# Spreading a first loop's loads over its instruction order, piece by piece, and shortening the warming ahead of the next loop

## The chip, the cores and the metric

The kernel runs on one core of one Trainium2 chip. A core has five engines that run side by side: TensorE (PE in the profile, with its weight loads as PEld), VectorE (DVE), ScalarE (ACT), GpSimd (POOL) and SyncE (SP), which here only issues DMAs. Each engine takes its instructions in the order in which the program gives them; between engines there are only semaphores. The metric is the time of one execution in microseconds (us) on the device, as the median of several runs.

## The reference

Two blocks in a row, in fp32. The first is a linear attention with a decaying state (RWKV-6). For each of 4 batches and 8 heads, over 768 steps of head dimension 48:

```python
for t in range(S):
    cur = einsum('bhd,bhe->bhde', u[None] * k[t], v[t])
    y[t] = einsum('bhd,bhde->bhe', r[t], state + cur)
    state = w[t][..., None] * state + einsum('bhd,bhe->bhde', k[t], v[t])
```

The second is a two-layer network on the 3072 tokens of width 384 that come out of it, with the exact gelu:

```python
h = x @ w_in            # 384 -> 2048
g = 0.5 * h * (1 + erf(h / sqrt(2)))
out = g @ w_out         # 2048 -> 384
```

The weights arrive as float64, so the kernel also converts them to fp32 on the chip.

## The kernel before, in words

**Tiles.** The work is cut into eight tiles of 384 steps (x = 0 to 7; two tiles for each batch). One pass of the outer loop, number x, does the attention of tile x, and beside it the network of tile x - 1. So the first pass, "the first loop" below, has attention alone, and it does it in two units, each with half of the heads, to start before all of its data is there. The second pass starts with the first h products (`first_mlp`, line 1084), each followed by a gelu on ACT (line 1086) that frees one of two PSUM banks which the h products use in turn.

**Order.** Nothing is scheduled by a tool. Every part of the kernel is a Python generator that emits a few instructions and yields; a string `PLAN[x]` says by its letters which generator goes on next. In pass 0 they are: "." and "s" the two units, "l" the loads, "c" the conversion of weights, "p" early conversion steps on ACT, "w" the load of the next tile's v, "f" the beginning of tile 1's attention, "x" the warming of TensorE. As every engine works in order, a letter's place fixes where its instructions stand on each engine.

**Loads.** SP issues nearly all of them, on one queue:
- `load_first` (line 274): tile 0's r, k, w, six DMAs of 384 KB, unit 0's three first. No mark.
- `load_v` (line 278): a tile's v in one DMA of 584 KB. All tiles share one buffer for it.
- `load_second` (lines 285, 286): tile 1's r, k, w in eight DMAs of 288 KB.
- `weight_in` (lines 322, 326, 327): a piece of the weights, 768 KB of float64, into one of five buffers `raw`. With `gate` it goes in three DMAs of 256 KB, without it in one.
- `load` (line 298): the r, k, w and v of later tiles.

**Marks.** In `load_second`, and in `weight_in` with its gate, each DMA is preceded by a memset of one column of its target on DVE. The DMA writes the same bytes, so it has to wait for the memset, and so it is issued not before DVE's order has come to that place. Everything behind it on SP waits too.

```python
nc.vector.memset(bufs[1][:, s.start:s.start + 1], 0.0)
dma.dma_start(out=bufs[1][:, s], in_=rkw[1, :, s])
```

**Conversion.** For a piece, three ACT instructions (lines 459, 460, 462, `prepare`) read `raw`; two DVE instructions (471, 475, `finish`) make the fp32 weights; then the load three pieces further on is issued without a mark. The second "p" of pass 0 prepares piece 2; this stands on ACT ahead of the first gelu.

**Ends of pass 0.** Unit 1's result goes from PSUM to SBUF on ACT (line 970), and from there in six small DMAs into xT (line 886, three issued by SP, three by ACT). Then tile 1 begins: sums on DVE (534), r times u on ACT (524, tile kx), products on PE (575). The warming is a set of bf16 matmuls on zeros (`keep_warm`, line 349), two times three of 512 columns, between those products.

Of the kernel before, what the change touches and what calls it, by code (L numbers as in the profile page):

```python
# [10 lines left out]
F32 = mybir.dt.float32  # L11
# [25 lines left out]
NC_SP = 8  # L37
HALFWAY = 2
PLAN = {
    0: "l.s....llsl.lssslslss.lc.l.slslls...ssss..lcs.s.s.l.ss..ss..sccs.c.s.llpssslw..cs.ffpccxx",  # L40
    1: (
        "swcs.clc.cs.wccscwcc.csccsw..cwlsccccccsc.cs.swcccc.ccc.s.cwlssccsclcs.cwss.lscccsw.c.cwcw"
        ".s..clw..lw..wwccc..cccc.scc.l.cslfccscfccw.fcffy.w.y..fw....ywyw..yyxxx.wyfxx..x.w..y.fyx"
# [149 lines left out]
def kernel(  # L193
# [9 lines left out]
    nc = tc.nc  # L203
# [12 lines left out]
    io = ctx.enter_context(tc.tile_pool(name="io", bufs=2))  # L216
# [8 lines left out]
    def pair(name):  # L225
        return pools["d"].tile([128, 2, BANK], F32, name=name, tag="d")

    def fewer_pairs():
        pairs_of_banks.close()
        pools["d"] = ctx.enter_context(tc.tile_pool(name="pe", bufs=2, space=PSUM))  # L230
        pools["u"] = ctx.enter_context(tc.tile_pool(name="pu", bufs=1, space=PSUM))
        for i in range(2):
            u = bank_u(i)
            nc.tensor.matmul(u, lhsT=zeros[:, 0:128], rhs=zeros, start=True, stop=True)
# [6 lines left out]
    def bank(name="o_ps", i=None):  # L241
        if i is None:
            i = turns[0]
            turns[0] = 1 - i
        return ps.tile([128, BANK], F32, name=name, tag=f"m{i}")
# [4 lines left out]
    loaded = {}  # L250

    def units_of(x):
        return NPART if x == 0 else 1
# [4 lines left out]
    bufs = [io.tile([128, 3 * NP * T], F32, name=f"rkw{i}", bufs=1) for i in range(2)]  # L258
# [7 lines left out]
    def load_first():  # L266

        t = bufs[0]
        loaded[0] = [None, None]
        size = 3 * NP * T // units_of(0)  # L270
        nc.scalar.dma_start(out=u_sb, in_=u)
        for i, part in ((0, 2), (0, 0), (0, 1), (1, 0), (1, 1), (1, 2)):
            s = slice(i * size + part * size // 3, i * size + (part + 1) * size // 3)
            nc.sync.dma_start(out=t[:, s], in_=rkw[0, :, s])

    def load_v(x, dma):
        loaded[x][1] = io.tile([128, v.shape[2]], F32, name="v_in", bufs=1)
        dma.dma_start(out=loaded[x][1], in_=v[x])

    def load_second(dma):  # L280

        loaded[1] = [None, None]
        for i in range(SHARES):
            s = slice(i * 3 * ALL // SHARES, (i + 1) * 3 * ALL // SHARES)
            nc.vector.memset(bufs[1][:, s.start:s.start + 1], 0.0)
            dma.dma_start(out=bufs[1][:, s], in_=rkw[1, :, s])
            yield

    def load(x, dma):

        if x >= NX:
            return
        loaded[x] = [None, None]
        for i in (0, 2, 1):
            t = bufs[x % 2 if i == 0 else 1]
            for j in range(3):
                a = i * ALL + j * ALL // 3
                dma.dma_start(out=t[:, a:a + ALL // 3], in_=rkw[x, :, a:a + ALL // 3])
                yield
        load_v(x, dma)  # L300
        yield
# [12 lines left out]
    def weight_in(i, gate=False):  # L314

        if i < len(pieces):
            dst, src = pieces[i]
            raws[i] = cv.tile([128, PIECE], I64, name="raw", bufs=AHEAD) if wide else None
            if wide:
                dst = raws[i].rearrange("p (a c) -> p a c", a=dst.shape[1])  # L320
            if not gate:
                nc.sync.dma_start(out=dst, in_=src)
                return
            for a in range(dst.shape[1]):
                if wide:
                    nc.vector.memset(dst[:, a].bitcast(U32)[:, 0:1], 0)
                nc.sync.dma_start(out=dst[:, a], in_=src[:, a])
                yield

    load_first()  # L330
    load_v(0, nc.sync)


    zeros = const.tile([128, BANK], BF16, name="zeros")
# [8 lines left out]
    def keep_warm(n, elsewhere=False, n_cols=BANK):  # L343
        if elsewhere:
            t = pair("warm")[:, 0]
        else:
            t = bank("warm")
        for _ in range(n):
            nc.tensor.matmul(t[:, 0:n_cols], lhsT=zeros[:, 0:128], rhs=zeros[:, 0:n_cols], start=True, stop=True)
# [698 lines left out]
    def h_sums(qs):  # L1048

        for q in qs:  # L1050
            for o, sign, a, b in FORMS_W:
                o, a, b = (of_q(w_block(z), q) for z in (o, a, b))
                (nc.vector.tensor_add if sign == "+" else nc.vector.tensor_sub)(o, a, b)
                yield
# [7 lines left out]
    def sums_of_x(x):  # L1062

        for o, sign, a, b in FORMS_X:
            o, a, b = (x_form(z) for z in (o, a, b))
            if sign == "n":
                nc.vector.scalar_tensor_tensor(out=o, in0=a, scalar=-1.0, in1=b, op0=ALU.mult, op1=ALU.subtract)
            else:
                (nc.vector.tensor_add if sign == "+" else nc.vector.tensor_sub)(o, a, b)
            yield  # L1070
# [7 lines left out]
    def first_mlp():  # L1078

        gs = [gp.tile([128, FG, T], F32, name="g") for _ in range(NF // FG)]  # L1080
        for f in range(NF):
            h_ps = bank("h_ps")[:, 0:T]
            for j in range(NJ):
                nc.tensor.matmul(h_ps, lhsT=w_in_sb[:, f // FI, j, f % FI * 128:(f % FI + 1) * 128], rhs=xT[:, j, :],  # L1084
                                 start=(j == 0), stop=(j == NJ - 1))
            nc.scalar.activation(out=gs[f // FG][:, f % FG], in_=h_ps, func=AF.Gelu)
            yield
        for blocks in (0, 1), (2,):
            o_ps = {i: bank()[:, 0:DM] for i in blocks}
            for f in range(NF):  # L1090
                for i, o in o_ps.items():
                    nc.tensor.matmul(o, lhsT=gs[f // FG][:, f % FG, i * 128:(i + 1) * 128], rhs=w_out_sb[:, f, :],  # L1092
                                     start=(f == 0), stop=(f == NF - 1))
                if f < NF - 1:
                    yield
            for i, o in o_ps.items():
                o_sb = wk.tile([128, DM], F32, name="o_sb", bufs=OUTS)
                nc.scalar.copy(out=o_sb, in_=o)
                store(i * 128, o_sb)
            yield  # L1100
# [139 lines left out]
    second = load_second(nc.sync)  # L1240
# [8 lines left out]
    def prepare_apart():  # L1249
        for i in range(2, 2 + HALFWAY):  # L1250
            prepare(i)
            yield

    def next_v():
        load_v(1, nc.sync)
        yield

    def warm():
        for _ in range(2):
            keep_warm(3, True)  # L1260
            yield

    def masks_and_sums():
        yield from make_quarter_masks()
        homes()
        yield from h_sums([0])
# [3 lines left out]
    for x in range(NX):  # L1270
        following = attention(x + 1, 0) if x + 1 < NX else iter(())
        if x == 0:
            streams = {
                ".": units[0], "s": units[1], "f": following, "c": pieces_of_w, "w": next_v(), "x": warm(),
                "p": prepare_apart(),
                "l": chain(weight_in(0, True), islice(second, 5), weight_in(1, True), second, weight_in(2, True)),
            }
        else:
            streams = {
                **(mlp(x - 1) if x > 1 else {".": first_mlp()}),  # L1280
                "s": slots, "f": following,
                "l": load(x + 1, nc.sync),
                "x": sums_of_x(x),
                "w": masks_and_sums() if x == 1 else chain(h_sums([1]), o_sums(EARLY, len(FORMS_O))) if x == 2 else iter(()),
                "y": o_sums(0, EARLY) if x == 1 else iter(()),
                "c": pieces_of_w if x == 1 else iter(()),
            }
        for c in PLAN[x]:
            next(streams[c], None)
        for c in ".slxwp" if x == 0 else ".slxwcy" if x == 1 else ".vgeoslxw":  # L1290
            while next(streams[c], streams) is not streams:
                pass
        slots = following
        if x == 1:
            fewer_pairs()
# [63 lines left out]
```

## Time and profile before

| what | value |
|---|---|
| median of 3 runs | 576.1 us (575.36 to 579.16) |
| the profiled execution | 577.52 us, span 575.7 us |
| PE busy | 551.3 us (96%) |
| DVE busy | 489.2 us (85%) |
| ACT busy | 334.1 us (58%) |
| PE's clock as granted | 1.00 |
| DMA, mean over the span | 108 GB/s; 303, 178 and 159 in the first three slices of 14.4 us |
| first h product on PE | 42.58 us |

The profile shows one execution, in microseconds from its start. A row of the timeline gives start, length, engine, line, operation, the tile written and the tiles read, and in brackets for how long the engine had been idle and what released it. "SPq" and "ACTq" rows are DMA issues, "issue" as a releaser means that the engine waited for nothing that the profile shows. The order of SP's issues in pass 0 is, with their starts: r, k, w of tile 0 (0.74 to 3.1), v (3.57), w_in piece 0 (4.51, 9.21, 9.63), five parts of tile 1 (10.10 to 15.36), w_in piece 1 (16.47 to 18.67), the other three parts of tile 1 (19.15, 24.44, 26.66), piece 3 without a mark (27.04), two parts of piece 2 (31.20, 31.63), three moves into xT (36.60), the third part of piece 2 (38.57), v of tile 1 (39.23).

### The profile page before, as it was taken

The page shows a single profiled execution, that of the slowest core. Times are in us where ns is not written, and L with a number is a line of the kernel's source. Part 1 is how long each engine was busy: PE and PEld are TensorE (multiplying, and loading weights), DVE is VectorE, ACT ScalarE, POOL GpSimd, SP SyncE. Part 2 cuts the span into 40 slices and gives each one's busy share as a digit, 9 for nine tenths or more (in the row PEclk, how much of TensorE's full clock was granted, in tenths as well). Part 3 has the DMA queues.
Part 4 walks back from the last instruction along what each step waited for, and adds up shares of the span by engine and source line. Part 5 has one row for each costly group of instructions (what it writes and reads, how often), then busy time and mean ns, then how long its engine had stood idle before and what let it go on. Part 6 is the DMA issues. An engine that isn't in the chain of part 4 may idle for free. (4 is left out here: it accounts for less than half of the span.)

```text
span 575.7 us, 17712 instructions
## 1 busy us (share of the span) xinstructions
PE 551.3 (96%) x7412; PEld 491.1 (85%) x7420; DVE 489.2 (85%) x977; ACT 334.1 (58%) x768; POOL 106.1 (18%) x105
## 2 busy tenths in 40 slices
PE   7689999999998999999999999999999999999997
PEld 4576665689998989999898998989898988999997
DVE  7889879999989989798989979799888989755464
ACT  2468995347753677347763477527772478535820
POOL 5100000016200460006400252005500072000000
PEclk9999999999999999999999999999999999999999
DMA  8559742239342782558623593337915384200001
GB/s 303 178 159 370 239 142 87 81 86 154 47 82 64 175 106 36 139 156 131 81 46 114 135 165 44 60 91 159 131 30 135 84 105 62 43 25 30 0 1 41
DMA packets 71646, 62.15 MB, mean 108 GB/s; under 512 B 32912, under 2 KB 56720, under 8 KB 71568
## 3 DMA queue, kind: packets, MB, share of 16 engines
q1 hardware_dynamic: 50112, 45.62, 26.4%
q0 software_dynamic: 21216, 15.34, 20.3%
q8 instruction: 58, 0.95, 0.7%
q14 instruction: 20, 0.16, 0.1%
q10 hardware_dynamic: 240, 0.08, 0.1%
HBM read 36.24 MB, written 4.72 MB: 71 GB/s over the span
## 5 line engine op out<-in xcount | busy, mean ns | idle before, releaser
L1148 POOL DMA_DIRECT2D g<-o_sb x78 | 94.9, 1490 | 370.7 <-ACT g L1117 347.2
L1197 DVE TENSOR_TENSOR g<-g 128x512 f32<-128x512 f32 x112 | 75.1, 688 | 24.3 <-PE o_ps L1073 21.3
L1117 ACT COPY o_sb<-u_ps 128x384 f32<-128x384 f32 (+1 forms) x56 | 25.8, 461 | 67.6 <-PE u_ps L1073 66.2
L1073 PE MATMUL h_ps<-forms_x,w_in_sb 128*128 128x192 f32 x280 | 57.7, 332 | 0.0
L1073 PE MATMUL o_ps<-w_out_sb,g 128*128 128x192 f32 x280 | 50.5, 327 | 0.5 <-DVE g L1197 0.5
L1117 ACT COPY g<-h_ps 128x384 f32<-128x384 f32 x84 | 40.4, 482 | 16.3 <-PE h_ps L1073 14.4
L1073 PEld LDWEIGHTS h_ps<-forms_x,w_in_sb 128*128 128x128 f32 x280 | 46.6, 190 | 2.7 <-ACT g L1117 2.2
L1073 PEld LDWEIGHTS o_ps<-w_out_sb,g 128*128 128x128 f32 x280 | 46.0, 190 | 1.2 <-DVE g L1197 0.8
L1166 ACT ACTIVATE g<-g 128x384 f32<-128x384 f32 x98 | 46.2, 519 | 0.3
L1073 PE MATMUL o_ps<-t,g 128*128 128x192 f32 x224 | 41.4, 328 | 0.1
L726 ACT COPY a_sb<-d 32x320 f32<-32x320 f32 (+5 forms) x108 | 39.3, 364 | 3.6 <-DVE a_sb L784 1.7
L1073 PEld LDWEIGHTS o_ps<-t,g 128*128 128x128 f32 x224 | 36.8, 190 | 0.7 <-PE u_ps L1073 0.3
L1073 PE MATMUL h_ps<-forms_x,s 128*128 128x192 f32 x168 | 35.5, 334 | 0.0
L1073 PE MATMUL h_ps<-xT,w_in_sb 128*128 128x192 f32 x168 | 35.0, 331 | 0.1
L710 PE MATMUL d<-kx,rkw 64*64 64x96 f32 x1152 | 32.0, 248 | 3.0 <-ACT a_sb L726 1.9
L710 PEld LDWEIGHTS d<-kx,rkw 64*64 64x64 f32 x1152 | 25.6, 133 | 9.6 <-issue 4.3
L1084 PE MATMUL h_ps<-xT,w_in_sb 128*128 128x384 f32 x96 | 33.0, 494 | 0.2
L1073 PE MATMUL u_ps<-xT,w_in_sb 128*128 128x192 f32 x168 | 32.5, 328 | 0.1
L1073 PE MATMUL u_ps<-w_out_sb,g 128*128 128x192 f32 x168 | 30.9, 332 | 1.4 <-ACT o_sb L1115 0.8
L1092 PE MATMUL o_ps<-w_out_sb,g 128*128 128x384 f32 x96 | 31.7, 489 | 0.0
L575 PEld LDWEIGHTS d<-rkw 64*64 64x64 f32 x1152 | 19.1, 134 | 14.2 <-issue 8.5
L739 DVE COPY_PREDICATED a_sb<-quarter,d 128x480 f32<-128x480 uint8 (+5 forms) x54 | 23.2, 440 | 8.7 <-PE d L710 7.4
(178 smaller groups left out, 1206.2 us busy)
## 6 DMA issues: line engine op xcount, KB each, us to landing
g<-o_sb POOLq DMA_DIRECT2D x78, 192.0 KB, 4.2
rkw<-in_rkw_dram SPq DMA_DIRECT2D x54, 256.0 KB, 3.7
raw<-in_w_out_dram SPq DMA_DIRECT2D x8, 768.0 KB, 5.4
v_in<-in_v_dram SPq DMA_DIRECT2D x8, 584.0 KB, 4.6
out_dram<-o_sb SPq DMA_DIRECT2D x24, 192.0 KB, 2.1
raw<-in_w_in_dram SPq DMA_DIRECT2D x5, 768.0 KB, 9.2
rkw<-kx SPq DMA_DIRECT2D x72, 48.0 KB, 2.1
rkw<-in_rkw_dram SPq DMA_DIRECT2D x6, 384.0 KB, 6.8
```

The source lines that it names most:

```text
L575: nc.tensor.matmul(d[half[p], g, n * width:(n + 1) * width], lhsT=kc[half[g], b, i, p], rhs=right(half[g], b, i, p), start=True, stop=True)
L710: nc.tensor.matmul(d[half[p], g, i * 3 * C // 2:(i + 1) * 3 * C // 2], lhsT=kc[half[g], n // NI, n % NI, p], rhs=rx[half[g], 2 * n + p], s ...
L726: nc.scalar.copy(out=at[z, g, first:behind, (a + 1) * h:], in_=d[z, :, :, to] if g == slice(None) else d[z, :, to])
L739: nc.vector.copy_predicated(out=an[:, :, :, :, (a + 1) * h:], mask=mask.to_broadcast(data.shape), data=data)
L1073: nc.tensor.matmul(o, lhsT=lhsT, rhs=rhs, start=start, stop=True, skip_group_check=True)
L1084: nc.tensor.matmul(h_ps, lhsT=w_in_sb[:, f // FI, j, f % FI * 128:(f % FI + 1) * 128], rhs=xT[:, j, :], start=(j == 0), stop=(j == NJ - 1))
L1092: nc.tensor.matmul(o, lhsT=gs[f // FG][:, f % FG, i * 128:(i + 1) * 128], rhs=w_out_sb[:, f, :], start=(f == 0), stop=(f == NF - 1))
L1117: nc.scalar.copy(out=o, in_=z)
L1148: nc.gpsimd.dma_start(out=o, in_=saved[q, t], accum_op=ALU.add)
L1166: nc.scalar.activation(out=o, in_=z, func=AF.Gelu, scale=MINUS.get(h, 1.0))
L1197: nc.vector.tensor_add(o, o, g_block(what[3:5]))
```

## The change

Three edits:
- v of tile 0 is no longer issued right behind r, k, w. It comes in two halves of 292 KB, each with a mark, out of the "l" stream, between w_in piece 0 and tile 1's r, k, w.
- The plan of pass 0 has two "l" more, and all of them stand elsewhere. The order of all other letters is the same: with the "l" taken out, both strings read alike. Counted in other letters that stand ahead of it, the loads are begun at:

| load | before | after |
|---|---|---|
| w_in piece 0, three parts | 0, 6, 6 | 6, 8, 11 |
| v of tile 0 | ahead of all | 12, 15 |
| tile 1, first five parts | 7, 8, 11, 12, 15 | 17, 19, 22, 24, 27 |
| w_in piece 1 | 17, 19, 20 | 30, 36, 38 |
| tile 1, last three parts | 20, 30, 37 | 41, 51, 55 |
| w_in piece 2 | 55, 55, 59 | 59, 62, 65 |

  "w", which loads tile 1's v, is letter 59 (so a load at 59 stands ahead of it, one at 62 behind), "p" are letters 55 and 67, "f" 65 and 66, and the "c" that issues piece 3 is 51.
- The warming in "x" takes 64 columns in place of 512.

```diff
-    0: "l.s....llsl.lssslslss.lc.l.slslls...ssss..lcs.s.s.l.ss..ss..sccs.c.s.llpssslw..cs.ffpccxx",
+    0: ".s....ls.lssslslss.lc.l.slss.l..lsssls..lcs.s.sl..lss.l.ss..sccs.lc.s.lpssslw..lcs.lffpccxx",
...
+    def first_v():
+        loaded[0][1] = t = io.tile([128, v.shape[2]], F32, name="v_in", bufs=1)
+        for i in range(2):
+            s = slice(i * v.shape[2] // 2, (i + 1) * v.shape[2] // 2)
+            nc.vector.memset(t[:, s.start:s.start + 1], 0.0)
+            nc.sync.dma_start(out=t[:, s], in_=v[0][:, s])
+            yield
+
     load_first()
-    load_v(0, nc.sync)
...
         for _ in range(2):
-            keep_warm(3, True)
+            keep_warm(3, True, 64)
             yield
...
-                "l": chain(weight_in(0, True), islice(second, 5), weight_in(1, True), second, weight_in(2, True)),
+                "l": chain(weight_in(0, True), first_v(), islice(second, 5), weight_in(1, True), second, weight_in(2, True)),
```

## The prediction

> **What bounds the kernel.** I read the stretches table first, then the waits of each engine, then the timelines of SP, ACT and PE around 36 to 50 us. In the stretches table a row is: stretch, its length, then busy time (and instructions) of PE, PEld, DVE, ACT and POOL, the granted clock, the DMA share and GB/s.
>
> ```profile
> 0.00:10.00 10.00, 7.42 (x146) 4.53 (x150) 5.92 (x30) 3.74 (x6) 5.09 (x16) 1.00 0.81 286
> 10.00:20.00 10.00, 6.94 (x276) 5.16 (x272) 8.95 (x19) 2.94 (x3) 6.12 (x11) 1.00 0.84 275
> 20.00:30.00 10.00, 7.23 (x308) 6.21 (x310) 8.75 (x15) 4.39 (x12) 0.00 (x0) 1.00 0.56 173
> 30.00:40.00 10.00, 7.99 (x371) 7.36 (x373) 8.68 (x37) 5.79 (x10) 0.00 (x0) 1.00 0.36 116
> 40.00:50.00 10.00, 10.00 (x214) 6.67 (x211) 9.78 (x17) 8.94 (x13) 0.00 (x0) 1.00 0.94 320
> 50.00:60.00 10.00, 10.00 (x135) 6.33 (x128) 9.83 (x14) 9.42 (x12) 0.00 (x0) 1.00 0.99 357
> ```
>
> Two regimes meet at 42.6 us. Before it (the first loop) DVE is nearly full and PE has holes. From 42.58 us, where the first h product starts, PE has none: asked for PE's waits between 42 and 110 us, the table of waits is empty, and the 18 h matmuls keep 6.07/18 = 0.337 us each. So a microsecond that PE loses there is lost to the end, and one that the first loop gains moves everything forward.
>
> What the first loop loses is in its waits (line, what it waited for: total us, times, longest), PE's from 8 to 40 us and DVE's from 8 to 36.6:
>
> ```profile
> PE d L575 <- issue: 2.9, 4, 1.5
> PE y_ps L865 <- issue: 1.4, 1, 1.4
> ...
> DVE rkw L617 <- issue: 0.8, 1, 0.8
> DVE rkw L628 <- PE d L575: 0.6, 2, 0.4
> DVE rkw L628 <- issue: 0.5, 1, 0.5
> ```
>
> PE stands still 4.3 us for "issue", and DVE 0.8 + 0.6 + 0.5 = 1.9 us behind it. The restarts after these stalls are PE's 701st, 955th, 1211th and 1723rd instruction, about 256 or twice that apart, and each comes 1.44 to 1.53 us after the end of one 16 KB packet of the "instruction" queue. So PE waits for its code. From a restart to the start of the next such packet passed 2.4 and 2.1 us where the DMA carried about 245 GB/s (packets at 15.62, 20.24), 1.35 us where it carried 89 (packet at 24.03).
>
> **Part 1: the early loads (v, w_in pieces 0 and 1, the second tile) are spread.** First tile's r, k, w stay first on SP's queue. In the packets, told apart by their sizes, v's begin at 8.41, when r, k, w are nearly through (last one ends 9.96): one queue serves in order, so taking v from behind them wins nothing for them. I cost that at 0. What needs v (PE at 29.89), raw piece 0 (ACT at 14.27, then nothing on ACT until 24.18) and raw piece 1 (ACT at 31.40, then idle 1.79 us) has room: the new marks stand some 3 us later at most for piece 0, and near 27 to 28.6 us for piece 1, which with the 3.2 us that a lone 256 KB piece took (31.20 to 34.36) lands by 31.9. The second tile's last eighth is still issued at 31.2, lands by about 36 and is wanted at 38.92. Piece 3 (768 KB, no mark) is queued on SP behind a mark and goes from 27.04 to about 29.7; wanted at 45.54. All hidden.
>
> What is left is the code fetch. By the new order about 1.4 MB falls into 13 to 21 us (177 GB/s, was 245) and 1.1 MB into 22 to 27 (200, was 89). A line through the rows above (0.9 us more delay for 156 GB/s more) gives 0.4 us less for two fetches, whose 0.45 and 0.41 us on DVE go; 0.65 us more for the third, which stands in DVE's 0.84; and perhaps 0.3 more near 32 us. Sum about **0**. Bounds: -1.9 (all DVE waits for PE's code go) and +2.0 (two quiet fetches become as late as the busy ones). I take 0, between rows that pull either way.
>
> [...]
>
> **Part 2: two marks more, v in two DMAs.** Marks beside other DVE work start 0.007 to 0.009 us apart (9.121, 9.130, 9.138), though each lasts 0.06: 0.02 to 0.12 us. SP gains one issue of 0.33 to 0.43 us where it waits for marks anyway. 0.
>
> **Part 3: short warming.** Five recorded of six matmuls last 1.47 us from 39.24, so about 40.6. Behind them PE's 96 matmuls on kx start at 40.64, but those wait for ACT's kx (L524), whose first ends 40.49. So the warming hides behind ACT: gain 0 to 0.1, and I take 0. Without that cover it would be worth 1.3.
>
> **Part 4: w_in piece 2 moves behind the next v on SP.** This is the term that counts. The letters: in the plan of before two of its three l stand ahead of "p" and the third ahead of "w"; in the new one the first stands ahead of "w" and two behind it, ahead of "f". SP issues in order. Before (SP's queue, then ACT, then PE; start, length):
>
> ```profile
> 31.20 1.68 SPq L327 DMA_DIRECT2D raw<-in_w_in_dram  x2
> 36.60 1.86 SPq L886 DMA_DIRECT2D xT<-ysb  x3
> 38.57 0.56 SPq L327 DMA_DIRECT2D raw<-in_w_in_dram  x1
> 39.23 1.23 SPq L278 DMA_DIRECT2D v_in<-in_v_dram  x1
> 40.51 0.43 SPq L322 DMA_DIRECT2D raw<-in_w_in_dram  x1
> ...
> 42.17 0.93 ACT L459 ACTIVATE f<-raw 128x768 f32<-128x768 f32 x1 [0.15 <-DMA raw<-in_w_in_dram]
> 42.99 1.01 ACT L460 ACTIVATE e<-raw,two 128x768 f32<-128x768 uint32 x1
> 44.03 1.10 ACT L462 ACTIVATE e<-raw 128x768 f16<-128x768 f32 x1
> 45.15 0.49 ACT L1086 ACTIVATE g<-h_ps 128x384 f32<-128x384 f32 x1
> ...
> 42.58 6.07 PE L1084 MATMUL h_ps<-xT,w_in_sb 128*128 128x384 f32 x18
> ```
>
> The third part of piece 2 is issued at 38.57, lands at 42.09, and ACT at 42.17 has just waited 0.15 us for it: no slack at all. Afterwards the *first* part takes the 38.57 slot (SP comes free of the xT moves then), v the 39.23 slot, and parts two and three (marks done by about 38.9) go out at 40.5 and 40.9, in the place of the transfer that left at 40.51. I read their landing from that transfer's packets. v's packets ran 41.11 to 44.61; the first 256 packets of 2 KB behind them (512 KB, just these two parts) had ended at 45.33. On the engine that finished v last, 16 packets of 0.092 us more end at 46.1. A landing came 0.35 us after the last packet (v: 44.61, 44.96). So 45.7 to 46.45; I take 46.1, **4.0 us later** than 42.09.
>
> Behind that wait on ACT stand three conversions (2.98 us) and then the gelu that frees the first of two PSUM banks. It ends at 45.64 now, at 49.65 then. PE's third h block wants that bank at 42.58 + 2 x 2.02 = 46.6. So PE stalls about **3.0 us** (2.65 to 3.4 by the two landings), where it had no wait. DVE's L471 (45.08, needs ACT's f) slips to about 47.1, but the copies behind it have those 3 us too. Following the engines on, the next bank's gelu ends near 53.1 and PE wants it at 53.25, so the shift is not doubled; nor given back, since ACT is over 9.4 of 10 us busy to 70 us. Later pieces land 1.5 us later (512 KB at 350 GB/s): the tightest that I see, issued at 41.52, landed at 50.73 for ACT at 53.66, and ACT moves too.
>
> **Sum.** 0 + 0 + 0 + 3.0 = +3.0 us. The profiled execution takes 577.52 (span 575.7), so 580.5 there; that execution lies 1.4 us over the median of the three runs (576.1), so against the median I forecast **579.1**, 0.5% slower.
>
> **Rivals.**
> (a) Not slower: parts two and three land beside v, not behind it. Needed is a landing before 42.17 + 0.98 = 43.15, as PE wants the bank 0.98 us after the gelu's present end. For it: v leaves room on the DMA (216 GB/s from 41 to 43 us, 354 from 45 to 47.5). Against: 2 KB packets started behind v's on each occasion. Then only Part 1 remains: 576.1, or 574.2 with its full gain. Chance 0.25.
> (b) Clearly slower: the stall costs PE its pace too. The first fp32 matmuls (L353, 512 wide) start 0.85 us apart, where the h pace scaled to 512 columns gives 0.45: near half speed early on. Full pace is there at 6.93, so the slow time is some 4 us; a relapse costs 2 us: 581.1. With a code fetch at its worst (+2.0) 583.1. Against: after the 1.46 us hole at 18.12 the matmuls are as short as before (0.21 us), clock 1.00 throughout; a 3 us hole is not in this trace. It decides if the hole grows past what the clock bears. Chance 0.11.
> [...]
> (c) Faster by more than 1%: no wait in the head is large enough (1.9 us at most against 5.8); left for what I have not seen. 0.04.
>
> **Numbers.** Forecast 0.60: 578.2 to 580.0. The range takes in most of (a) and the mild end of (b): 575.2 to 581.3. One per cent, 5.8 us, is about what a measurement of this kernel can tell from no change (its three runs lie 3.8 us apart). Faster 0.04; within 0.87 (the forecast, (a) and the mild part of (b)); slower 0.09.
>
> **What would show it.** ACT L459 waiting about 4 us for the DMA of raw near 42 us; PE's h_ps waiting about 3 us for ACT g L1086 near 47; SP's queue with v_in between parts of raw; the kx matmuls still waiting for ACT L524 after a short warming; the first loop's end within 2 us of 42.6. Wrong would be: no ACT wait there, or "issue" waits that change by more than 2 us.

## The result, and the profile after

The changed kernel is slower: a median of 585.2 us (six executions, 582.68 to 587.79) against 578.7 us for the kernel before (six, 575.36 to 581.92). The ratio is 1.0115 with a 95% interval of 1.0066 to 1.0165. The profiled execution took 582.68 us (span 580.9), 5.2 us more than the one of before in both; it is the fastest of the six.

Where it went is seen by setting the same PE weight load of both traces side by side (its start after, minus its start before):

| at, before (us) | 21.0 | 25.1 | 30.5 | 34.6 | 38.6 | 48.6 | 84.6 | 288.8 | 437.5 | end |
|---|---|---|---|---|---|---|---|---|---|---|
| later by (us) | -1.60 | -1.33 | -0.78 | +1.58 | +1.69 | +6.85 | +6.33 | +6.15 | +5.59 | +5.2 |

So PE is early by 1.6 us at 21 us, loses 2.4 us between 30 and 35, and 5.2 between 39 and 49. Then the kernel keeps its distance; half a microsecond comes back by 85 us and some more in small steps to the end.

The stretches table of the changed kernel (stretch, length; busy time of PE, PEld, DVE, ACT, POOL; granted clock, DMA share, GB/s):

```profile
0.00:10.00 10.00, 6.59 (x150) 4.47 (x155) 6.50 (x28) 3.73 (x6) 5.16 (x16) 1.00 0.70 243
10.00:20.00 10.00, 7.68 (x319) 5.65 (x313) 9.96 (x19) 2.92 (x3) 5.99 (x11) 1.00 0.59 186
20.00:30.00 10.00, 6.99 (x306) 6.26 (x309) 8.65 (x22) 5.67 (x14) 0.00 (x0) 1.00 0.77 223
30.00:40.00 10.00, 6.45 (x275) 6.31 (x271) 5.27 (x29) 3.42 (x5) 0.00 (x0) 0.83 0.38 130
40.00:50.00 10.00, 7.51 (x176) 5.52 (x169) 7.54 (x16) 3.24 (x7) 0.00 (x0) 0.83 0.71 220
50.00:60.00 10.00, 8.18 (x117) 4.97 (x116) 9.14 (x12) 9.88 (x14) 0.00 (x0) 1.00 0.99 365
```

From 10 to 20 us DVE is now full (9.96, was 8.95): the early gain. From 30 to 60 us PE has 7.9 us of holes (it had 2.0), and the granted clock, 1.00 in every one of these rows before, is 0.83 in two of them. Cut along the changes of the clock that the trace records, the same view is:

```profile
31.51:34.92 3.41, 0.06 (x3) 0.00 (x0) 2.98 (x19) 1.43 (x2) 0.00 (x0) 1.00 0.66 233
34.92:38.33 3.41, 3.21 (x85) 3.21 (x88) 0.29 (x3) 0.00 (x0) 0.00 (x0) 0.50 0.02 5
38.34:41.75 3.41, 2.97 (x151) 2.81 (x147) 2.46 (x6) 0.48 (x1) 0.00 (x0) 1.00 0.08 19
41.75:45.16 3.41, 1.36 (x69) 1.23 (x72) 3.20 (x11) 2.98 (x6) 0.00 (x0) 1.00 0.64 177
45.17:48.57 3.40, 3.40 (x44) 2.35 (x37) 2.66 (x3) 0.10 (x1) 0.00 (x0) 0.50 0.98 320
```

Two stretches of 3.41 us at half clock, each right behind a stretch of 3.41 us in which PE stood still for most of the time. PE's timeline (start, length, engine, line, operation, tiles, count, idle time before and its releaser; behind the new function all lines are 7 higher than before) names the holes:

```profile
31.35 0.22 PE L872 MATMUL y_ps<-a_sb,v_in 64*64 64x64 f32 x1
35.12 1.54 PE L872 MATMUL y_ps<-a_sb,v_in 64*64 64x64 f32 x45 [3.55 <-issue]
36.35 0.31 PE L901 MATMUL y_ps<-rkw,st 64*64 64x64 f32 x1
36.36 0.31 PE L872 MATMUL y_ps<-a_sb,v_in 64*64 64x64 f32 x1
36.46 3.09 PE L901 MATMUL y_ps<-rkw,st 64*64 64x64 f32 x77
39.34 0.25 PE L582 MATMUL d<-rkw 64*64 64x32 f32 x2
39.39 0.22 PE L901 MATMUL y_ps<-rkw,st 64*64 64x64 f32 x2
39.42 1.61 PE L582 MATMUL d<-rkw 64*64 64x32 f32 x94
40.96 0.35 PE L356 MATMUL warm<-zeros 128*128 128x64 bf16 x6
43.80 2.44 PE L582 MATMUL d<-kx,rkw 64*64 64x64 f32 x96 [2.49 <-ACT kx L531]
46.17 5.31 PE L1091 MATMUL h_ps<-xT,w_in_sb 128*128 128x384 f32 x12
53.30 2.20 PE L1091 MATMUL h_ps<-xT,w_in_sb 128*128 128x384 f32 x6 [1.82 <-ACT g L1093]
```

Three holes: 3.55 us for "issue" (PE's code: the packet of the instruction queue came at 32.73 to 33.69, PE went on 1.43 us after its end); 2.49 us ahead of the products on kx, where the short warming (0.35 us) leaves off; 1.82 us for the gelu of the first h block. The 12 h matmuls, in part at half clock, take 5.31 us, against 4.05 at the earlier pace. Before, the first hole was 1.39 us, and the second and third were none:

```profile
33.98 0.86 PE L865 MATMUL y_ps<-a_sb,v_in 64*64 64x64 f32 x44 [1.39 <-issue]
39.24 1.47 PE L349 MATMUL warm<-zeros 128*128 128x512 bf16 x5
40.64 2.01 PE L575 MATMUL d<-kx,rkw 64*64 64x64 f32 x96
```

ACT's side of the third hole (same columns):

```profile
43.13 2.14 ACT L531 ACTIVATE kx<-rkw,u_sb 128x384 f32<-128x384 f32 x4
49.84 0.90 ACT L466 ACTIVATE f<-raw 128x768 f32<-128x768 f32 x1 [4.58 <-DMA raw<-in_w_in_dram]
```

This is the wait that I predicted, 4.58 us long. The queue of SP shows why, with v between the parts of raw:

```profile
42.07 0.53 SPq L327 DMA_DIRECT2D raw<-in_w_in_dram  x1
42.69 0.38 SPq L278 DMA_DIRECT2D v_in<-in_v_dram  x1
43.16 0.86 SPq L327 DMA_DIRECT2D raw<-in_w_in_dram  x2
```

So the open question is the other part: is the late piece all that counts, or do the code wait and the half clock cost on their own? And what makes the code late?

### The profile page after: what moved, and what is told of

It is laid out like the page before. It is cut to its first block, busy times and chain, and to the rows that moved or that the text cites. A ratio compares the mean times of both kernels' runs of the same rounds, so it can differ in the third digit from the quotient of the medians.

```text
span 580.9 us, 17718 instructions
## 1 busy us (share of the span) xinstructions
PE 551.4 (95%) x7413; PEld 492.4 (85%) x7420; DVE 489.7 (84%) x979; ACT 333.0 (57%) x768; POOL 106.1 (18%) x105
## 4 chain that ended last, share of the span: by engine, by line
PE 72%; DVE 14%; ACT 7%; issue 4%; DMA 2%; SPq 0%; ACTq 0%; DVEq 0%
PE u_ps L1080 20%; PE o_ps L1080 17%; PE h_ps L1080 14%; PE o_ps L1099 5%; PE h_ps L1091 5%; DVE a_sb L746 3%; PE kv_ps L831 2%; DVE st L846 2%; ACT a_sb L733 2%; PE d L582 2%; PE d L717 2%; PE y_ps L901 2%; PE y_ps L931 1%; DVE a_sb L791 1%; DVE kx L693 1%
## 5 line engine op out<-in xcount | busy, mean ns | idle before, releaser
L1124 ACT COPY o_sb<-u_ps 128x384 f32<-128x384 f32 (+1 forms) x56 | 25.7, 459 | 67.7 <-PE u_ps L1080 66.2
L1091 PE MATMUL h_ps<-xT,w_in_sb 128*128 128x384 f32 x96 | 34.2, 507 | 1.8 <-ACT g L1093 1.8
L746 DVE COPY_PREDICATED a_sb<-quarter,d 128x480 f32<-128x480 uint8 (+5 forms) x54 | 23.1, 439 | 8.7 <-PE d L717 7.4
L846 DVE SCALAR_TENSOR_TENSOR st<-st,tot_sb,kv_ps 128x48 f32<-128x48 f32 x160 | 29.0, 258 | 1.5 <-PE kv_ps L831 1.3
```

Of the source, the lines that this page charges most:

```text
L746: nc.vector.copy_predicated(out=an[:, :, :, :, (a + 1) * h:], mask=mask.to_broadcast(data.shape), data=data)
L846: nc.vector.scalar_tensor_tensor(out=stq[:, q, c], in0=stq[:, q, c - 1] if c else b4[:, q, NC - 1], scalar=totq[:, q, c:c + 1], in1=kvs[q ...
L1124: nc.scalar.copy(out=o, in_=z)
```

## Experiments

Each run is compared with 20 to 34 executions of the kernel before, run beside it (the change itself with six). "Later at 48.6" is the PE weight load of the table above in the one profiled execution, against the one profiled execution of before. Up to 25 us e1, e3 and e7 execute what the kernel before executes, and still lie 0.2 to 0.6 us off: so much is scatter between executions.

| run | what | ratio (95% interval) | later at 25.1 | at 34.6 | at 48.6 |
|---|---|---|---|---|---|
| the change | all three edits | 1.0115 (1.0066 to 1.0165) | -1.33 | +1.58 | +6.85 |
| e1 | piece 2 alone | 1.0077 (1.0052 to 1.0102) | -0.56 | +1.09 | +4.26 |
| e2 | early loads alone | 1.0071 (1.0046 to 1.0095) | -1.23 | +1.77 | +2.61 |
| e3 | short warming alone | 1.0015 (0.9987 to 1.0042) | -0.18 | -0.15 | +0.36 |
| e4 | the change, long warming | 1.0120 (1.0095 to 1.0145) | -1.41 | +1.55 | +6.89 |
| e5 | the change, piece 3 late | 1.0082 (1.0054 to 1.0110) | -1.53 | +0.12 | +5.90 |
| e6 | the change, piece 2 ahead of v | 1.0086 (1.0061 to 1.0111) | -1.44 | +2.34 | +5.81 |
| e7 | before, with a burst | 1.0051 (1.0026 to 1.0076) | -0.56 | +1.78 | +4.16 |
| e8 | spread | 0.9999 (0.9971 to 1.0027) | -1.73 | -0.90 | +1.50 |
| e9 | timed | 1.0029 (1.0001 to 1.0058) | -1.45 | +0.17 | +2.09 |
| e10 | timed, short warming | 1.0042 (1.0012 to 1.0073) | -0.85 | +0.90 | +2.08 |

### e1: piece 2 alone

```diff
 # kernel before
-    0: "... .c.s.llpssslw..cs.ffpccxx",
+    0: "... .c.s.pssslw..lcs.lffpccxx",
```

> The kernel before with one edit: the three loads of w_in piece 2 begin at letters 59, 62, 65, two of them behind the next tile's v. Theory 'late piece' (the wait that I predicted is what costs): ACT L459 waits 3.6 to 4.4 us for raw near 42 us, PE waits 2.7 to 3.4 us for the gelu near 47 us, and the whole is 3.0 us slower (0.5%), with the first loop as it was (first h product within 0.3 us of 42.58). Rival 'code and clock' (what costs lies ahead of h, in the long code wait at 31.4 us and in two stretches of half clock that the changed kernel's trace shows): the wait on ACT is there, but most of the loss is missing, under 1.5 us.

Slower by 0.77%, 4.4 us. Its ACT and PE timelines:

```profile
47.26 0.91 ACT L459 ACTIVATE f<-raw 128x768 f32<-128x768 f32 x1 [4.22 <-DMA raw<-in_w_in_dram]
...
31.34 0.62 PE L824 MATMUL kv_ps<-v_in,kx 64*64 64x48 f32 x28 [1.19 <-issue]
...
44.18 4.14 PE L1084 MATMUL h_ps<-xT,w_in_sb 128*128 128x384 f32 x12
50.71 2.20 PE L1084 MATMUL h_ps<-xT,w_in_sb 128*128 128x384 f32 x6 [2.39 <-ACT g L1086]
```

ACT waits 4.22 us. By the starts, the third h block is 6.53 us behind the first, which was 3.97 before: 2.6 us, and the delay grows by 2.9 from 38.6 to 48.6 us. "Late piece" holds for that step. But h itself starts 1.6 us late (44.18, forecast 42.58 within 0.3): by 30.5 us this execution had lost 1.65 since 25, and at 31.34 it had waited 1.19 us for code, for a packet that started only 2.9 us after the block before it had begun. That is not the edit: the first mark that it moves stood at 31.12 in the kernel before, and up to there both execute the same instructions. What differs is less than half a microsecond of timing. Here an eighth of tile 1 was issued at 26.09 and PE began its block at 26.12; in the trace of before PE began it at 26.41, the eighth was issued behind that, at 26.66, and the packet came after 1.09 us. So the trace shows the forecast 3 us as the edit's own, and the measured 4.4 are not fully accounted for. Four of the six executions had a mean clock of 0.994 or less, of the kernel before none of 20, so half clock behind the wait is likely a part; this was not shown.

### e2: the early loads alone

```diff
 # the changed kernel
-    0: "... .lc.s.lpssslw..lcs.lffpccxx",
+    0: "... .lc.s.lllpssslw..cs.ffpccxx",
...
-            keep_warm(3, True, 64)
+            keep_warm(3, True)
```

> The changed kernel with piece 2 back at letters 55, 55, 59 and with the long warming: only the early loads are spread. Theory 'late piece': little is left of the loss, under 1.5 us against before, and no wait of ACT for raw near 42 us. Rival 'code and clock': PE is 1.3 to 1.6 us early at 20 to 25 us, then waits 3 to 4 us for 'issue' near 31.4 us as the changed kernel did, and is at half clock for one stretch of 3.4 us after it; h starts about 3 us late and the whole is about 3 us slower. With the piece 2 loads issued where they were, behind the same burst, I expect the rival's code wait here.

Slower by 0.71%, 4.1 us (3.3 by the medians), with ACT's wait for raw down to 1.0 us. PE's timeline, and the stretch at half clock that follows:

```profile
35.74 0.86 PE L872 MATMUL y_ps<-a_sb,v_in 64*64 64x64 f32 x44 [4.10 <-issue]
```

```profile
36.89:40.30 3.41, 3.41 (x86) 3.41 (x85) 1.11 (x2) 0.48 (x1) 0.00 (x0) 0.50 0.00 0
```

"Code and clock" holds: 1.2 us gained by 25 us, 3.0 lost to the code, 0.6 more at half clock. With e1 this makes two losses of about 4 us, each there without the other; together (e4) they cost 1.20%, against a sum of 1.48%, which the intervals do not tell apart.

### e3: the short warming alone

```diff
 # kernel before
-            keep_warm(3, True)
+            keep_warm(3, True, 64)
```

> The kernel before with the warming at 64 columns and nothing else. Both theories of the loads: 0, as PE's 96 products on kx wait for ACT's kx at 40.5 us anyway, and PE is idle for about 1.0 us (39.6 to 40.6) in place of warming. Theory 'clock': if a hole of 1.0 us is enough for a stretch of half clock, h runs at half pace for 3.4 us and the whole is 1.3 to 1.7 us slower.

The interval includes no change. The profiled execution had no half clock. The executions scatter, though: 5 of 12 had a mean clock of 0.994 or less (a stretch of 3.41 us at half clock is 0.003 of 580 us, so two or more), of the kernel before in that batch none of 20. Beside the runs e5 to e8, on another chip, six of 34 executions of the kernel before had it too, so this is a tendency at most. Whether those stretches lie ahead of h was not seen, as only the first execution is profiled.

### e4: the change with the long warming

```diff
 # the changed kernel
-            keep_warm(3, True, 64)
+            keep_warm(3, True)
```

> The changed kernel with the long warming. If the half clock from 45.2 us on in the changed kernel comes from the hole of 2.7 us that the short warming leaves ahead of h (41.1 to 43.8), the clock stays at 1.00 there, the hole shrinks to 1.4 us or less, and the first h products keep 0.34 us each in place of 0.44. The gain in time is small all the same, 0 to 0.5 us, since PE's third h block waits for ACT's gelu behind piece 2 in either case: PE's wait for that gelu grows from 1.8 to about 3.4 us. Rival: that half clock is all that counts at this place, and the kernel is 1.6 us faster than the changed one.

The time is the changed kernel's (585.33 us). The hole ahead of the products on kx shrinks to 1.7 us (1.4 or less expected) and the second stretch at half clock is gone, but PE then waits 3.3 us for the gelu in place of 1.8. So in these two traces the half clock from 45.2 us on goes with the short warming and costs nothing there: it hides behind the late piece.

### e5: piece 3 behind piece 2

```diff
 # the changed kernel
-        for _ in weight_in(i + 3):
+        for _ in weight_in(i + 3) if i else ():
...
-    0: "... w..lcs.lffpccxx",
+    0: "... w..lcs.llffpccxx",
...
-                "l": chain(..., weight_in(2, True)),
+                "l": chain(..., weight_in(2, True), weight_in(3)),
```

> The changed kernel with one edit: w_in piece 3 (768 KB) is issued behind piece 2, at letter 65, and no longer at 28.5 us. Theory 'burst' (a packet of PE's code waits behind the loads that were queued when PE asked for it; in the changed kernel these are an eighth of tile 1 and piece 3, and the packet starts 3.3 us after PE has come to its 1455th instruction): the packet starts by 31 us, PE's wait for 'issue' near 31.4 us falls from 3.6 us to 1.5 us or less, no half clock follows at 35 us, and unit 0 ends about 3 us earlier. The wait of ACT for raw piece 2 stays, so the whole is 2.5 to 3.5 us faster than the changed kernel (+0.5 to +0.7% against before). Rival 'own pace' (PE waits because it has run ahead of its code, whatever the loads): the wait stays over 3 us and the time is the changed kernel's.

The code packet starts at 31.26 (was 32.73), the wait falls to 2.18 us, no half clock follows, and at 38.6 us the run is 1.85 us ahead of the changed kernel. "Burst" has the direction right and the size wrong: I expected a wait of 1.5 us at most and a gain of 2.5 to 3.5. The median, 582.98, lies 2.2 us under the changed kernel's, measured beside other executions, and the intervals overlap. In the trace it loses most of its lead again:

```profile
42.72 4.14 PE L1091 MATMUL h_ps<-xT,w_in_sb 128*128 128x384 f32 x12
50.85 3.70 PE L1091 MATMUL h_ps<-xT,w_in_sb 128*128 128x384 f32 x6 [4.00 <-ACT g L1093]
```

h starts at 42.72, nearly as early as before the change; the wait for the late piece grows to 4.00 us, and a stretch at half clock follows it, so the next six matmuls take 3.70 us. Here the rival (b) of the prediction is seen as it was told, the clock lost in the hole of the late piece.

### e6: piece 2 ahead of v

```diff
 # the changed kernel
-    0: "... .lc.s.lpssslw..lcs.lffpccxx",
+    0: "... .lc.s.lpssslllw..cs.ffpccxx",
```

> The changed kernel with one edit: all three loads of w_in piece 2 at letter 59, ahead of the next tile's v on SP, still behind the moves into xT. If being behind v is what makes piece 2 late, it lands some 3.3 us after its last issue at about 43 us, so at 46.3, and ACT's wait for raw falls from 4.6 us to about 1.0; PE's wait for the gelu goes; the whole is 2 us or more faster than the changed kernel, with the code wait at 31.4 us as there. If being behind the moves into xT is enough to make it late, the wait on ACT stays over 2.5 us.

```profile
48.53 0.96 ACT L466 ACTIVATE f<-raw 128x768 f32<-128x768 f32 x1 [1.67 <-DMA raw<-in_w_in_dram]
```

ACT's wait for raw falls from 4.58 to 1.67 us (and 0.3 once more; 1.0 expected), PE's wait for the gelu goes, and the median is 583.22, 2.0 us under the changed kernel's (not measured side by side, and the intervals overlap). Part of that fall is only that ACT comes to piece 2 later, at 46.86 in place of 45.27. Counted from where SP has done the moves into xT and issues the first part (42.85, in the changed kernel 42.07), ACT has the piece 5.7 us later, with v in between 7.8, and 3.6 in the kernel before, where one part alone stood behind the moves. So some 2.1 us of the lateness come from standing behind v, and as much from standing behind the moves into xT. The code wait was 4.4 us here and gave two stretches of half clock in a row (35.0 to 41.8).

### e7: a burst in the kernel before

```diff
 # kernel before
-    0: "... .lcs.s.s.l.ss..ss..sccs.c.s.llpssslw..",
+    0: "... .lcs.s.s..ss..ss..sccs.lc.s.llpssslw..",
```

> The kernel before with one edit: the last eighth of tile 1 begins at letter 51 in place of 37, and piece 3 behind it on SP with it, so that both are issued at about 29.3 us, shortly ahead of the point near 30.3 us where PE asks for code. Theory 'burst': the code packet that started at 31.36 starts at about 33, PE's wait for 'issue' at 34 us grows from 1.4 to 3 us or more, a stretch of half clock can follow, and the whole is 1.5 to 3 us slower. Rival 'own pace': PE's wait stays within 0.5 us of 1.4 and the time is that of before.

One letter is moved: an eighth of tile 1, and with it piece 3, go out at 28.25 and 28.63 us in place of 26.66 and 27.04. Apart from the one-column mark on DVE that moves with it, no compute instruction is touched.

```profile
31.21 0.29 PE L865 MATMUL y_ps<-a_sb,v_in 64*64 64x64 f32 x2
35.31 1.44 PE L865 MATMUL y_ps<-a_sb,v_in 64*64 64x64 f32 x44 [3.81 <-issue]
...
36.65 4.01 PE L894 MATMUL y_ps<-rkw,st 64*64 64x64 f32 x77
```

```profile
34.39:41.20 6.81, 5.89 (x156) 5.89 (x158) 1.92 (x6) 0.48 (x1) 0.00 (x0) 0.50 0.06 15
```

The packet starts at 33.07 (about 33 expected), the wait is 3.81 us, two stretches of half clock follow, and it costs 0.51%, 2.9 us. This settles it for "burst" against "own pace".

It can be told in one table. A block of PE's code begins with the 1468th matmul or weight load in the trace (the 1474th where the trace holds six records more; the texts written ahead of the runs call it the 1455th, and the next block's first the 1711th); from it to the start of the next packet of code passes, against what SP had issued by then and no packet had yet moved:

| run | before | e3 | e1 | e8 | e9 | e10 | e5 | the change | e2 | e4 | e6 | e7 |
|---|---|---|---|---|---|---|---|---|---|---|---|---|
| queued, KB | 324 | 430 | 24 | 270 | 277 | 259 | 248 | 1034 | 1049 | 1040 | 988 | 1056 |
| packet starts after, us | 1.11 | 1.21 | 1.12 | 1.39 | 1.42 | 1.31 | 1.44 | 3.26 | 3.78 | 3.40 | 4.05 | 3.95 |

Five runs with a megabyte queued: 3.3 to 4.1 us. Seven with less than half of one: 1.1 to 1.4. The KB alone are not all of it: at the earlier block of e1 told above 305 KB cost 2.9 us, as most had only just been issued; the last of them began to move at 28.44, and the packet started at 29.02.

### e8, e9, e10: towards a faster version

```diff
 # e8, from the changed kernel: piece 3 into the "l" stream as in e5, long warming, and
-    0: "... .lc.s.lpssslw..lcs.lffpccxx",
+    0: "... .lc.s.lplslslslw..cs.ffpccxx",
 # e9, from e8
-    0: "... .l.ss..sccs.lc.s.lplslslslw..cs.ffpccxx",
+    0: "... .ll.ss..sccs.c.s.lplllssslw..cs.ffpccxx",
 # e10 is e9 with keep_warm(3, True, 64)
```

> The changed kernel with the early loads where they are, the long warming, piece 2 at letters 56, 57, 58 (ahead of the moves into xT) and piece 3 at 59 (behind them, ahead of the next v): the early loads keep what they gain, and no burst stands ahead of PE's code near 29.5 us. Theories 'late piece' and 'burst' together: code wait near 31.4 us at most 1.5 us, clock at 1.00, no wait of ACT for raw over 0.5 us, first h product at about 41.5 us (42.6 before), the whole 0.5 to 1.5 us faster than before. If something else in the spread loads costs time, it is slower than before.

The code wait at 31.2 us is 1.63 (1.5 at most expected) and ACT does not wait for raw; yet the time is that of before (0.9999), not 0.5 to 1.5 us better. PE's timeline shows the next block of code late in its turn:

```profile
33.08 0.86 PE L872 MATMUL y_ps<-a_sb,v_in 64*64 64x64 f32 x44 [1.63 <-issue]
...
37.91 2.30 PE L582 MATMUL d<-rkw 64*64 64x32 f32 x94 [1.66 <-issue]
```

The block ahead of it begins at 33.08, behind the parts of piece 2 issued at 32.32 and 32.74, and its packet came 2.5 us later. A stretch of half clock (38.5 to 41.9) follows, and the 0.9 us in hand at 34.6 become 1.5 lost at 48.6.

> The arrangement of the run before (early loads as in the change, long warming, piece 3 behind the moves into xT), with two shifts so that little is queued where PE asks for code: the seventh eighth of tile 1 at letter 41 in place of 51, and all of piece 2 at letter 56. Theory 'burst': at PE's 1455th instruction (about 29.4 us) under 200 KB are queued and the code packet starts within 1.3 us; at the 1711th (about 33 us) under 150 KB are queued, the packet starts within 1.4 us instead of 2.5, and the second hole (1.9 us near 37 us) shrinks under 0.8 us. So no half clock before 45 us, h at about 41.5 us, the whole 0.5 to 1.5 us faster than before. Rival 'no room' (every order of these loads delays some code packet): another wait for 'issue' of over 1.5 us shows up elsewhere before h, and the time is that of before or slower.

The second hole went, but the first grew to 2.18 us and took the clock with it (34.0 to 37.4). I had misjudged the queue: 277 KB at the first block, not under 200, and 480 KB where the next block begins, not under 150, where the packet took 1.7 us. It is 0.29% slower than before (the interval just leaves out no change), so "no room" is nearer the truth: every order that I tried left a code wait of 1.6 us or more at this place. There may be a floor under it, an estimate from the smallest figures of these traces: with almost nothing queued a packet started 1.1 us after its block began, the shortest took 0.9, and PE went on about 1.45 after its end. That makes 3.5 us at best, while PE with the spread loads runs through that block in 2.1 us (e8: 29.35 to 31.45), so some 1.4 us of wait would be left; the kernel before had 1.39. It does not explain all of e8: of the 1.7 us that it was early at 25 us, 0.8 were gone by 30.5, none went at this wait (-0.90 at 30.5 and at 34.6), and 1.3 went between 34.6 and 38.6, at the next block.

> The same with the warming at 64 columns. If the short warming only does harm where PE stands still ahead of h for another reason (2.7 us in the changed kernel), it costs nothing here (within 0.3 us of the long one) and the clock stays at 1.00 ahead of h. If the hole that it leaves is enough in some executions, as the spread of the run with the short warming alone suggests (5 of 12 executions at a mean clock of 0.994 or less, none of the 20 of the kernel before), the median is 1 to 2 us above the long warming's, and the mean clocks lie lower.

580.37 against 578.88 us for the long warming; the two intervals overlap. 7 of 12 executions had a mean clock of 0.994 or less, 2 of 12 with the long warming. Together with e3 this speaks for the hole mattering in some executions, but the time of it, about 1.5 us, is not settled.

## Why the prediction was wrong

I forecast 579.1 us, +3.0 us; it is 585.2, +6.5 us against the 578.7 us measured beside it. The sign was right, the size was half of what came. Of the 6.1 us between forecast and result 2.6 are the kernel before itself, whose median was 576.1 in the three runs that I had and 578.7 in six; the other 3.5 are terms of the sum.

- **Part 4, piece 2 behind v: right.** Forecast: ACT waits 4.0 us, PE 3.0. Measured: 4.58 in the changed kernel, 4.22 alone (e1); of PE's loss 2.6 to 2.9 us in e1. In the changed kernel PE's own wait is 1.82; with the long warming and h at full clock it is 3.3 (e4). e6 shows the cause as far as v goes, some 2.1 us; about as much comes from standing behind the moves into xT, which the forecast's issue order had in it as well.
- **Part 1, early loads: the step that failed.** Forecast 0, bounds -1.9 and +2.0. Measured alone (e2): +4.1 us (3.3 by the medians). The term in it that was mis-sized is the fetch "near 32 us": put at perhaps 0.3 us more, its wait grew by 2.2 (1.39 to 3.55) in the changed kernel and by 2.7 in e2 (4.10), and the half clock behind it was not in the sum at all. Three things were wrong in it. I drew a line through the mean GB/s of a stretch, where at this block the delay goes with what lies queued at the moment when PE begins it (the table at e7). I had read that piece 3 slips from 27.0 to about 29.7 (it was 28.5; piece 1, put at 27 to 28.6, went out from 23.1 to 25.7) and called it hidden, as the piece itself was in time: its cover for ACT held, but it stood ahead of PE's code. And my upper bound was the latest of the packets that I had looked at (2.4 us). The trace of before itself holds one that starts 4.4 us after its block was begun (41.31 to 45.66, with 1.3 MB queued); I passed over it, since nobody waits for it there, where an h matmul takes 0.34 us against 0.02 of the small ones on kx. The gain was real: -1.6 us by 21 us.
- **The clock was priced only in a rival.** Rival (b), chance 0.11, put the half clock behind the late piece. In the profiled execution it came behind the code wait, on the first loop's last products on the state (L894: 2.32 us before, 3.09 after), and together with the longer issue of the moves into xT (2.20 us on ACT's queue before, 2.88 after) it turned 1.69 us into 3.16 at the products on kx; how much of that is the clock's was not separated. Behind the late piece it is seen in e5. I had argued from "clock 1.00 throughout", which one execution showed: of the 77 of the kernel before that ran beside e1 to e10, 34 had a mean clock of 0.997 or less, which is a stretch of 3.41 us or more at half clock.
- **Part 3, short warming.** The cover that I named, ACT's kx, held and even grew (2.49 us). What I did not see is that the hole so left can set the clock for h (0.50 from 45.17 to 48.57 us in the changed kernel). It costs nothing in the changed kernel (e4), and perhaps 1.5 us elsewhere (e3, e10; not settled).
- **Part 2, two more marks:** nothing in the traces speaks against 0.
- **Rival (a)**, parts two and three beside v, falls with e1 and e6.
- "Later than 42.6 by 2 us at most" for the first loop's end was wrong: h began at 46.17.

How long a hole the clock bears was open in rival (b). That 3 us were safe was my estimate and was not shown: the longest hole of PE in the trace of before was 1.46 us from 8 us on, with the clock at 1.00 behind it. In the runs holes of some 2 us were enough for half clock, and every half clock up to the first h blocks lasted 3.41 us or twice that: see the last section.

## To carry to other kernels

In these runs PE's code came in DMA packets of 16 KB, and among matmuls of 0.02 us each PE stood still for it for up to 4.4 us (e6). Where a kernel has such waits, look in the packets of the instruction queue how long after the start of a block each one starts, and keep large transfers from being queued shortly ahead of that start. Here this has only avoided the loss (e8 ran as fast as before); no order was found that gains. When a transfer moves, price its effect on everything that shares the queue at that moment, not only on who reads it. And a hole on PE is to be priced with the pace behind it (a granted clock of 0.50 for 3.41 us behind ten stretches of these traces), not with its length alone, and from more than one execution.

## What the runs showed of the hardware

- **Holes of some 2 us in all were enough for half clock.** The changes of the clock in the twelve traces lie on a grid of 3.41 us. From the first record of full clock (4.2 to 7.2 us) up to the first h blocks, behind each cell in which PE stood still for 1.9 us or more in all, ten of them, the next cell ran at half clock (1.91, 1.98, 2.05 and 2.18 us among them). Two cells that already ran at half clock were followed by another, though PE idled only 0.87 and 0.92 us in them (e6, e7). Cells with 1.63 to 1.83 us kept the clock, but for one of 1.66 (e8). A hole of 2.4 us that fell across two cells (e1: 1.11 and 1.28) left the clock alone, one of 2.2 us within one cell (e9) did not. As the grid lies elsewhere in each trace (its first record at 4.20 us in the changed kernel, at 6.53 in the kernel before), whether a hole of some 2 us cost the clock was in part chance here. The mean clocks of the changed kernel's six executions, 0.988 to 0.996, differ as this would have it.
- **PE's code came later with more data queued.** The code packets have a queue of their own, and still started 3.3 to 4.1 us after a block had begun with about 1 MB queued by SP (the change, e2, e4, e6, e7), 1.1 with 24 KB (e1). When the code packet started, most of what had been queued as the block began was on its way: in the kernel before 154 of 162 packets (code packet at 31.36, the last of them at 31.96), in the changed kernel all 118 of tile 1 and 354 of the 384 of piece 3 (code packet at 32.73, the last of them at 33.84). Where 2 MB and more were queued, around 43 us, the code packet came well ahead of the end of what was queued (e8: 2.8 MB gone at 50.2, packet at 47.04). What the order is stays open.
